# Attention and top-1 experts on one core: the common slots' rows gathered earlier and turned later

## The chip, the cores and the metric

The kernel runs on one core of a Trainium2 chip. The metric is device time in microseconds of one execution. TensorE, VectorE, ScalarE and GpSimd each work through their own list of instructions in order; SyncE and the others also issue transfers, which run on 16 DMA engines that the core's queues share.

## The reference

Attention with a memory term for 4 batches of 576 tokens and 8 heads of 64 gives x, 2304 rows of 512. Then each row goes to one of 8 experts:

```
logits = x @ w_gate;  e_idx = argmax(logits, axis=1)
for e in range(E):
    mask = e_idx == e
    h = maximum(x[mask] @ w1[e], 0)           # 512 -> 1024
    ye = h @ w2[e]                            # 1024 -> 512
    out[mask] = gate_w[mask] * eom[mask, e] * ye
```

## The kernel before

The first part (to about 226 us) computes attention and routing and writes the rows x to `xs` and their gates to `gd`, both in device memory. The second part works on **slots**: 128 rows that go to the same expert, 17 slots (`NMAIN`) in the main loop at line 1637. The change lies in that loop.

A slot `s` passes through these steps. `gather(s)` (L1365) fetches its rows from `xs` with an indirect DMA that GpSimd issues. `stage_x(s)` (L1372) turns them on TensorE (four transposes into the PSUM tile `px`, L1376), ScalarE copies them twice (`xh` rounded, `x32` as it is, L1381 and L1383), and GpSimd takes the difference `xl` (L1384). `gemm1(s)` (L1414) is the first product: 24 matmuls in four pieces `c` of six, each out of `whi*xh`, `whi*xl` and `wlo*xh` (L1405), then relu on ScalarE. `stage_h(s)` (L1421) turns the result with eight transposes (`hp`) and splits it into `hh` and `hl`, the latter again on GpSimd (L1436). `gemm2(s)` (L1439) is the second product, 24 matmuls into `py`, and an activation that weighs with the gate into `y`, one of two buffers. `scatter(s)` (L1458) writes the rows out with an indirect DMA from GpSimd. `gemm` takes a function `mid`, which it calls before the third piece, in the middle of the product (L1394): this is how transposes get into a product.

Beside the slots there are two **common slots**, numbered `kind` 0 and 1. Each holds rows of several experts: kind 0 has four groups of 32 rows, kind 1 two groups of 64, and each group is multiplied by its own expert's weights on a part of the array. `group_gather(kind)` (L1547) fetches the rows into `xc` and the gates into `gk`, two indirect DMAs of GpSimd. `group_turn(kind)` (L1554) turns the rows on TensorE (four transposes into `pc`, which takes the same PSUM buffer as `px`), and ScalarE copies them to `cx`. The work on them is cut into 24 `unit`s (L1563; the matmuls are at L1584, `ch` and `cy`), of which one follows each product from slot 2 on. Their weights come in transfers that ScalarE issues, into two buffers (`wide_load`, L1522); a unit waits for its transfer with a semaphore, and a buffer is filled again when its unit is done.

The order is written out by hand. On TensorE a pass `s` of the loop does: first product of slot `s + 1`, turn of slot `s + 2`, a unit, second product of slot `s` (with the turn `hp` of slot `s + 1` in its middle), a unit. The table `plan` (L1606) says what is put at a point `(s, half)`, after the first or the second half of pass `s`, or at `(s, "mid")`, in the middle of the first product of slot `s`. GpSimd's list follows the order in which the code calls it: at a pass's end `gather(s + 4)`, `scatter(s)`, and in passes 0 and 7 `group_gather`. The experts' weights are fetched by SyncE and split by VectorE (`load_expert`, L1335), which waits until the products of an earlier expert are done.

```
    plan[1, 1] = [lambda: group_turn(0)]
        ...
        if s + 4 < NMAIN:
            gather(s + 4, False)
        scatter(s)
        if s in (0, 7):
            group_gather(s // 7)
```

Of the kernel before, what the change touches and what calls it, by code (L numbers as in the profile page):

```python
# [10 lines left out]
F32 = mybir.dt.float32  # L11
# [9 lines left out]
P = 128  # L21
# [111 lines left out]
def attn_moe(ctx: ExitStack, tc: tile.TileContext, qk, vd, mz, mt, rz, beta, wgo, w1, w2, out):  # L133
# [236 lines left out]
    def raw_tile(name, width=F):  # L370
        tag = ("qk", "qk", "hi", "hi", "hi")[turns[0] % 5]
        turns[0] += 1
        return kq.tile([P, width], F32, name=name, tag=tag, bufs=3 if tag == "hi" else 2)
# [708 lines left out]
    for item in ORDER:  # L1082
        name, _, eng = item.partition(":")
# [168 lines left out]
    mk = fin["mk"] = ctx.enter_context(tc.tile_pool(name="mk", bufs=1, side="right"))  # L1252
# [100 lines left out]
    def gather_gate(s):  # L1353
        g = st[s]["g"] = mk.tile([P, 1], F32, name=f"g{s}", tag="g", bufs=4)
        G.indirect_dma_start(out=g, out_offset=None, in_=gd[:MID if s == "e" else NT + 1], in_offset=bass.IndirectOffsetOnAxis(ap=slot_rows(s), axis=0))
# [16 lines left out]
    def stage_x(s):  # L1372
        t = st[s]
        px = pm.tile([P, 512], F32, name=f"px{s}", tag="px")
        for c in range(4):
            T.transpose(px[:, c * P:(c + 1) * P], t["x"][:, c * P:(c + 1) * P], ident)  # L1376
        if s == 1:
            xh, xl = (mk.tile([P, DM], F32R, name=f"x{n}1", tag="y", bufs=2) for n in "hl")
        else:
            xh, xl = (mk.tile([P, DM], F32R, name=f"x{n}{s}", tag=f"x{n}") for n in "hl")  # L1380
        A.copy(xh, px)  # L1381
        x32 = mk.tile([P, DM], F32, name=f"x32_{s}", tag="x32")
        A.copy(x32, px)  # L1383
        G.tensor_tensor(xl, x32, f32(xh), op=ALU.subtract)  # L1384
        t["x1"] = xh, xl

    def regs(s):
        st[s]["need"] = T.value_load(need[0:1, s:s + 1], min_val=0, max_val=8 * E)
        st[s]["par"] = T.value_load(pari[0:1, s:s + 1], min_val=0, max_val=1)
# [24 lines left out]
    def gemm1(s, mid=None):  # L1414
        h = pa.tile([P, F], F32, name=f"h{s}", tag="h")
        gemm(s, [h[:, :512], h[:, 512:]], st[s]["x1"], 0, 2, mid)
        h32 = st[s]["h"] = bq.tile([P, F], F32, name=f"h32_{s}", tag="h32")
        A.activation(h32, h, AF.Relu)  # L1418
        done(s, sem_1)
# [38 lines left out]
    def scatter(s):  # L1458
        i = G.indirect_dma_start(out=out, out_offset=bass.IndirectOffsetOnAxis(ap=outi[:, s:s + 1] if s < NMAIN else fin["outf"][:, s - NMAIN:s - NMAIN + 1], axis=0), in_=st.pop(s)["y"], in_offset=None, bounds_check=NT - 1, oob_is_err=False)
        if s == NMAIN - 2:  # L1460
            tc.add_to_no_dep_group("rows", i.ins)


    def split(e, c, eng):
        high(e, c, eng)
        low(e, c)
        ready()
# [44 lines left out]
    cst = {}  # L1512
# [5 lines left out]
    def numbers(g0, g1):  # L1518
        for g in range(g0, g1):
            cst["e", g] = A.value_load(groupi[0:1, g:g + 1], min_val=0, max_val=E - 1)  # L1520
# [26 lines left out]
    def group_gather(kind):  # L1547
        xr = mk.tile([P, DM], F32, name=f"xc{kind}", tag="xc")
        G.indirect_dma_start(out=xr, out_offset=None, in_=xs[:NT + 1], in_offset=bass.IndirectOffsetOnAxis(ap=group_row[:, kind:kind + 1], axis=0))
        g = mk.tile([P, 1], F32, name=f"gk{kind}", tag="gk", bufs=2)  # L1550
        G.indirect_dma_start(out=g, out_offset=None, in_=gd[:NT + 1], in_offset=bass.IndirectOffsetOnAxis(ap=group_row[:, kind:kind + 1], axis=0))
        cst[kind, "x"], cst[kind, "g"] = xr, g

    def group_turn(kind):  # L1554
        px = pm.tile([P, 512], F32, name=f"pc{kind}", tag="px")
        for c in range(4):
            T.transpose(px[:, c * P:(c + 1) * P], cst[kind, "x"][:, c * P:(c + 1) * P], ident)
        if "cx" not in cst:
            cst["cx"] = raw_tile("cx")
        x = cst[kind, "cx"] = cst["cx"]  # L1560
        A.copy(x[:, :512], px)

    def unit(u):  # L1563
        kind, part, k, count = loads[u]
        b = u % 2
        T.wait_ge(sem_c[b], count)
        ng = HALVES if kind else QUARTERS
        w = P // ng
        wt = wide[b].rearrange("p (g f) -> p g f", g=ng)
        if part == 0:  # L1570
            if k == 0:
                cst[kind, "h"] = [pa.tile([P, 512], F32, name=f"ch{kind}_{n}", tag=f"c{n}") for n in range(2)]
            todo = [(cst[kind, "h"][n], k, slice(n * 512, n * 512 + 512), k == 0, k == 3) for n in range(2)] if kind else [(cst[kind, "h"][k % 2], k // 2, slice(0, 512), k < 2, k >= 6)]
            x = cst[kind, "cx"]
        else:
            if k == 0:
                cst[kind, "y"] = pa.tile([P, DM], F32, name=f"cy{kind}", tag="c0")
            o = cst[kind, "y"]
            todo = [(o, 2 * k + n, slice(n * 512, n * 512 + 512), 2 * k + n == 0, 2 * k + n == 7) for n in range(2)] if kind else [(o, k, slice(0, 512), k == 0, k == 7)]
            x = cst[kind, "cT"]  # L1580
        for o, c, z, first, last in todo:
            for g in range(ng):
                r = slice(w * g, w * g + w)
                i = apart(T.matmul(o[r], x[:, c * P + w * g:c * P + w * g + w], wt[:, g, z], start=first, stop=last, tile_position=(0, w * g)))  # L1584
        return i

    def group_relu(kind):
        x = cst[kind, "h32"] = bq.tile([P, F], F32, name=f"ch32_{kind}", tag="h32")
        for n in range(2):
            A.activation(x[:, n * 512:n * 512 + 512], cst[kind, "h"][n], AF.Relu)  # L1590

    def group_h(kind):
        hp = pa.tile([P, F], F32, name=f"chp{kind}", tag="hp")
        for f in range(8):
            T.transpose(hp[:, f * P:(f + 1) * P], cst[kind, "h32"][:, f * P:(f + 1) * P], ident)
        x = cst[kind, "cT"] = cst["cx"]
        for n in range(2):
            A.copy(x[:, n * 512:n * 512 + 512], hp[:, n * 512:n * 512 + 512])

    def group_out_rows(kind):  # L1600
        y = mk.tile([P, DM], F32, name=f"yc{kind}", tag="y", bufs=2)
        A.activation(y, cst[kind, "y"], AF.Copy, scale=cst[kind, "g"])
        G.indirect_dma_start(out=out, out_offset=bass.IndirectOffsetOnAxis(ap=group_out[:, kind:kind + 1], axis=0), in_=y, in_offset=None, bounds_check=NT - 1, oob_is_err=False)

    loads = [(0, part, k) for part in range(2) for k in range(8)] + [(1, part, k) for part in range(2) for k in range(4)]
    plan = {}  # L1606
    for i in range(24):
        s, half = divmod(i, 2)
        plan[2 + s, half] = [lambda u=i: (unit(u), None)[0]]
    plan[1, 1] = [lambda: group_turn(0)]  # L1610
    plan[5, 1].append(lambda: group_relu(0))
    plan[7, "mid"] = lambda: group_h(0)
    plan[9, 1] += [lambda: group_out_rows(0), lambda: group_turn(1)]
    plan[11, 1].append(lambda: group_relu(1))
    plan[13, "mid"] = lambda: group_h(1)
    plan[13, 1].append(lambda: group_out_rows(1))
# [2 lines left out]
    def point(s, half):  # L1619
        last = None  # L1620
        for f in plan.get((s, half), ()):
            last = f() or last
        return last

    def refill(s, half):
        if (s, half) in plan and ahead[0] < len(loads) and s >= 2:
            wide_load(ahead[0])
            ahead[0] += 1
# [8 lines left out]
    for s in range(NMAIN):  # L1637
        if 0 < s < NMAIN - 1:
            gemm1(s + 1, plan.get((s + 1, "mid")))
        if s + 2 < NMAIN:  # L1640
            stage_x(s + 2)
            regs(s + 2)
        if s == 0:
            gather_gate(0)
            wide_load(0)
        if s < NMAIN - 1:
            gather_gate(s + 1)
        if s == NMAIN - 1:
            finish(s)
            break  # L1650
        i = point(s, 0)
        refill(s, 0)
        gemm2(s, lambda: (group_rows() if s == 0 else None, stage_h(s + 1)))
        i = point(s, 1) or i
        refill(s, 1)
        if s == 13:
            tc.declare_fence(i.ins, group="wide")
        if s % 4 == 3:
            G.drain()
        if s + 4 < NMAIN:  # L1660
            gather(s + 4, False)
        scatter(s)
        if s in (0, 7):
            group_gather(s // 7)
        if s == 0:
            wide_load(1)
            for c in range(8):
                fetch(1, c)
                split(1, c, V)
        if s == 8:  # L1670
            numbers(QUARTERS, GROUPS)
        if s < NPOS - 2:
            load_expert(s + 2)
# [101 lines left out]
```

## Time and profile before

| | |
|---|---|
| median of 3 runs | 484.91 us (484.63 to 485.42) |
| profiled execution | 484.58 us |
| its span | 482.9 us |
| mean granted clock of TensorE | 0.989 |
| busy share: TensorE, VectorE, ScalarE, GpSimd | 96%, 58%, 54%, 55% |

The span runs from the first to the last instruction; all times within it count from its start. The profiled execution is one of its own, beside the three runs, and 1.68 us of its time lie outside the span. An engine is busy while it executes; waits for a semaphore are idle time, and the view of waits puts each down to what ended it. The chain is followed back from the last instruction. "Issue" is idle time that ended without a visible wait. The DMA engines' share can read a little over 1.

### The profile page before, as it was taken

The numbers are of one execution on the slowest core, as the hardware profiler recorded it, in microseconds if no ns is written. First come the engines' busy times: TensorE is split into PE (matmuls) and PEld (weight loads), VectorE is DVE, ScalarE is ACT, GpSimd is POOL, SyncE is SP. The second block draws the span as 40 slices with busy tenths as digits, with TensorE's granted clock in tenths as the row PEclk, the third lists the DMA queues.
The fourth block names the chain that finished last, engine by engine and source line by source line (L and its number), as shares of the span: only waits on it lengthen the run. The fifth ranks groups of instructions, "written<-read, shape, count | busy, mean of one in ns | idle before, by whom it ended". The sixth has DMA issues, their size and how long they took to land.

```text
span 482.9 us, 10479 instructions
## 1 busy us (share of the span) xinstructions
PE 465.7 (96%) x3315; PEld 348.3 (72%) x3315; DVE 282.1 (58%) x847; ACT 262.6 (54%) x621; POOL 266.2 (55%) x264
## 2 busy tenths in 40 slices
PE   7999999999999999989996999999999999999994
PEld 4777877877877877646885677676676767676884
DVE  4978998989789978888995707007079700000000
ACT  5989898888878766345342423344233332523341
POOL 8846585544745742634587445454478653452452
PEclk9999999999999999999997999999999999999998
DMA  7544256243221271151598686858779745341001
GB/s 252 178 137 138 74 183 198 80 133 142 87 90 35 92 224 48 55 197 48 179 367 294 202 286 209 317 168 266 263 247 369 278 142 209 132 159 59 36 22 40
DMA packets 34215, 80.09 MB, mean 166 GB/s; under 512 B 4820, under 2 KB 5352, under 8 KB 34154
## 3 DMA queue, kind: packets, MB, share of 16 engines
q1 hardware_dynamic: 17610, 44.05, 27.3%
q10 hardware_dynamic: 12688, 25.30, 15.3%
q0 software_dynamic: 3856, 9.98, 6.0%
q8 instruction: 32, 0.52, 0.5%
q14 instruction: 29, 0.24, 0.1%
HBM read 69.86 MB, written 9.97 MB: 165 GB/s over the span
## 4 chain that ended last, share of the span: by engine, by line
PE 88%; DVE 3%; DMA 2%; issue 2%; ACT 1%; POOL 1%; POOLq 0%; SPq 0%; DVEq 0%; ACTq 0%
PE h L1405 20%; PE py L1405 17%; PE po L675 9%; PE pt L640 8%; PE s L565 7%; PE me L731 4%; PE cy L1584 3%; PE ch L1584 3%; PE hp L1431 3%; PE sd L552 3%; PE pt L609 2%; DMA xc<-xs,group_row 1%; PE px L1376 1%; PE pv L794 1%; PE pl L899 1%
## 5 line engine op out<-in xcount | busy, mean ns | idle before, releaser
L1436 POOL TENSOR_TENSOR hl<-hT,hh 128x512 fp32r<-128x512 f32 x32 | 45.8, 1454 | 52.1 <-ACT hh L1435 52.1
L628 ACT ACTIVATE st<-st,nm 128x128 f32<-128x128 f32 (+3 forms) x128 | 71.5, 562 | 3.5 <-DVE nm L623 3.2
L1098 DVE CAST whi<-kept 128x1024 fp32r<-128x1024 f32 x32 | 32.7, 1022 | 67.4 <-ACTq L1412 59.8
L623 DVE CUSTOM_DVE_ANT_0 st<-s,mask 128x128 f32<-128x128 f32 (+3 forms) x128 | 58.3, 483 | 9.4 <-PE s L565 5.4
L1405 PE MATMUL h<-whi,xh 128*128 (+1 forms) x136 | 56.7, 417 | 0.0
L460 POOL TENSOR_TENSOR lo<-qk,hi 128x1216 fp32r<-128x1216 f32 x15 | 42.2, 2811 | 23.2 <-ACT hi L456 17.7
L1405 PE MATMUL h<-whi,xl 128*128 (+1 forms) x136 | 54.0, 397 | 0.0
L487 ACT COPY PT<-pt 128x512 f32<-128x512 f32 (+2 forms) x89 | 45.3, 523 | 15.9 <-PE pt L640 13.8
L1405 PE MATMUL h<-wlo,xh 128*128 (+1 forms) x136 | 53.9, 396 | 0.0
L1405 PE MATMUL py<-whi,hh 128*128 (+1 forms) x128 | 53.0, 414 | 0.0
L1418 ACT ACTIVATE h<-h 128x1024 f32<-128x1024 f32 x17 | 17.4, 1026 | 63.5 <-PE h L1405 63.5
L1405 PE MATMUL py<-wlo,hh 128*128 (+1 forms) x128 | 50.2, 392 | 0.0
L1405 PE MATMUL py<-whi,hl 128*128 (+1 forms) x128 | 50.0, 391 | 0.0
L675 PE MATMUL po<-PT,v 128*64 128x320 f32 (+4 forms) x480 | 49.1, 349 | 0.8 <-ACT oT_hT L487 0.4
L640 PE MATMUL pt<-ident,st 128*128 128x128 f32 x320 | 47.7, 280 | 0.1
L1434 ACT COPY hT<-hp 128x512 f32<-128x512 f32 x34 | 20.1, 590 | 49.6 <-PE hp L1431 49.6
L1384 POOL TENSOR_TENSOR xl<-x,xh 128x512 fp32r<-128x512 f32 x17 | 23.5, 1383 | 41.6 <-ACT x L1383 40.6
L1101 DVE TENSOR_TENSOR wlo<-kept,whi 128x1024 fp32r<-128x1024 f32 x32 | 45.1, 1411 | 1.1
L675 PEld LDWEIGHTS po<-PT,v 128*64 128x64 f32 x480 | 29.6, 137 | 17.7 <-issue 2.8
L640 PEld LDWEIGHTS pt<-ident,st 128*128 128x128 f32 x320 | 35.2, 141 | 7.1 <-issue 1.9
L1435 ACT CAST hh<-hp 128x512 fp32r<-128x512 f32 x32 | 19.1, 596 | 32.3 <-PE py L1405 32.3
L1405 PEld LDWEIGHTS h<-whi,xh 128*128 128x128 f32 x136 | 26.1, 192 | 14.6 <-ACT hh L1435 9.1
(337 smaller groups left out, 1025.3 us busy)
## 6 DMA issues: line engine op xcount, KB each, us to landing
kept<-in_w SPq DMA_DIRECT2D x32, 512.0 KB
wide<-in_w ACTq DMA_DIRECT2D x64, 256.0 KB
qk<-in_qk SPq DMA_DIRECT2D x15, 640.0 KB
wide<-in_w ACTq DMA_DIRECT2D x16, 512.0 KB
v<-in_vd SPq DMA_DIRECT2D x16, 320.0 KB
xs<-xd SPq DMA_DIRECT2D x12, 256.0 KB
star<-in_w SPq DMA_DIRECT2D x6, 512.0 KB
mz<-in_mz SPq DMA_DIRECT2D x4, 324.0 KB
```

The lines of the kernel that those rows point to most:

```text
L460: G.tensor_tensor(c["lo"][:, TQ:], c["raw"][:, TQ:], f32(c["hi"])[:, TQ:], op=ALU.subtract)
L487: (A.copy if e == "ACT" else V.tensor_copy)(dst(), src())
L565: T.matmul(c()["ss", q][j], l[r, lc], m[r, KC:KC + w], start=(a == 0), stop=(a == 2))
L623: V.tensor_tensor_reduce(st[:, :w], c()["ss", qt][j], mask[:, 512 - w:512], -SCALE, 3.0e38, ALU.add, ALU.min, negm()[:, i:i + 1])
L628: A.activation(st, st, AF.Exp, bias=c()["negm"][:, i:i + 1], scale=-1.0, accum_out=sums()[:, qt, 2 * p + j:2 * p + j + 1])
L640: T.transpose(pt[:, (m * k1 + i) * P:(m * k1 + i + 1) * P], st[:, i * P:(i + 1) * P], ident)
L675: T.matmul(po[64 * j:64 * j + 64, qs - q0:q1 - q0], vt[:, k, 64 * j:64 * j + 64], PT[:, j, k, qs:q1], start=(k == 0), stop=(k == kn - 1))
L1098: join((A.copy if eng is A else eng.tensor_copy)(whi[:, e % 2, c, :], raws[e, c]))
L1101: join(eng.tensor_tensor(wlo[:, e % 2, c, :], raws.pop((e, c)), f32(whi[:, e % 2, c, :]), op=ALU.subtract))
L1405: i = T.matmul(o[n % nh], l[:, z], m[:, n * 512 + part.start:n * 512 + part.stop], start=(c == 0 and k == 0 and n < nh), stop=(c == 3 and ...
L1436: G.tensor_tensor(hl[:, z], hT[:, z], f32(hh)[:, z], op=ALU.subtract)
L1584: i = apart(T.matmul(o[r], x[:, c * P + w * g:c * P + w * g + w], wt[:, g, z], start=first, stop=last, tile_position=(0, w * g)))
```

## The change

In passes 0 and 8 (before: 0 and 7) the rows of a common slot are gathered first in the pass's list of GpSimd, ahead of `gather(s + 4)`. Their gates are gathered by a function of their own, two passes later, in passes 2 and 10. Slot 0's scatter moves from the end of pass 0 into pass 1, behind `stage_x(3)`. The turns move from the end of passes 1 and 9 into the middle of the first products of slots 3 and 11, which passes 2 and 10 begin with. No instruction is added or removed.

```diff
--- before.py
+++ after.py
@@ -1547,9 +1547,11 @@
     def group_gather(kind):
         xr = mk.tile([P, DM], F32, name=f"xc{kind}", tag="xc")
         G.indirect_dma_start(out=xr, out_offset=None, in_=xs[:NT + 1], in_offset=bass.IndirectOffsetOnAxis(ap=group_row[:, kind:kind + 1], axis=0))
-        g = mk.tile([P, 1], F32, name=f"gk{kind}", tag="gk", bufs=2)
+        cst[kind, "x"] = xr
+
+    def group_gate(kind):
+        g = cst[kind, "g"] = mk.tile([P, 1], F32, name=f"gk{kind}", tag="gk", bufs=2)
         G.indirect_dma_start(out=g, out_offset=None, in_=gd[:NT + 1], in_offset=bass.IndirectOffsetOnAxis(ap=group_row[:, kind:kind + 1], axis=0))
-        cst[kind, "x"], cst[kind, "g"] = xr, g
 
     def group_turn(kind):
         px = pm.tile([P, 512], F32, name=f"pc{kind}", tag="px")
@@ -1607,10 +1609,11 @@
     for i in range(24):
         s, half = divmod(i, 2)
         plan[2 + s, half] = [lambda u=i: (unit(u), None)[0]]
-    plan[1, 1] = [lambda: group_turn(0)]
+    plan[3, "mid"] = lambda: group_turn(0)
     plan[5, 1].append(lambda: group_relu(0))
     plan[7, "mid"] = lambda: group_h(0)
-    plan[9, 1] += [lambda: group_out_rows(0), lambda: group_turn(1)]
+    plan[9, 1].append(lambda: group_out_rows(0))
+    plan[11, "mid"] = lambda: group_turn(1)
     plan[11, 1].append(lambda: group_relu(1))
     plan[13, "mid"] = lambda: group_h(1)
     plan[13, 1].append(lambda: group_out_rows(1))
@@ -1640,6 +1643,8 @@
         if s + 2 < NMAIN:
             stage_x(s + 2)
             regs(s + 2)
+        if s == 1:
+            scatter(0)
         if s == 0:
             gather_gate(0)
             wide_load(0)
@@ -1657,11 +1662,14 @@
             tc.declare_fence(i.ins, group="wide")
         if s % 4 == 3:
             G.drain()
+        if s in (0, 8):
+            group_gather(s // 8)
         if s + 4 < NMAIN:
             gather(s + 4, False)
-        scatter(s)
-        if s in (0, 7):
-            group_gather(s // 7)
+        if s:
+            scatter(s)
+        if s in (2, 10):
+            group_gate(s // 8)
         if s == 0:
             wide_load(1)
             for c in range(8):
```

GpSimd's list at the end of pass 0, before. `xr` are a slot's gathered rows (slot 4 here), `out<-y` is a scatter, `xc` and `gk` are the common slot's rows and gates, `g` a slot's gate, `xl` and `hl` the differences.

```order
L1436 TENSOR_TENSOR hl_4000<-hT_3998,hh_3999 128x512 x2
L1367 DMA xr_4032<-xs,rowi_3514 128x512
L1459 DMA out<-y_4029,outi 2304x512
L1549 DMA xc_4037<-xs,group_row 128x512
L1551 DMA gk_4039<-gd,group_row 128x1
L1384 TENSOR_TENSOR xl_4180<-x_3_4182,xh_4179 128x512
L1355 DMA g_4203<-gd,rowi_3513 128x1
L1436 TENSOR_TENSOR hl_4224<-hT_4222,hh_4223 128x512 x2
```

The same place after the change:

```order
L1436 TENSOR_TENSOR hl_4000<-hT_3998,hh_3999 128x512 x2
L1549 DMA xc_4032<-xs,group_row 128x512
L1367 DMA xr_4034<-xs,rowi_3514 128x512
L1384 TENSOR_TENSOR xl_4175<-x_3_4177,xh_4174 128x512
L1459 DMA out<-y_4029,outi 2304x512
L1355 DMA g_4201<-gd,rowi_3513 128x1
L1436 TENSOR_TENSOR hl_4222<-hT_4220,hh_4221 128x512 x2
L1367 DMA xr_4252<-xs,rowi_3514 128x512
L1459 DMA out<-y_4249,outi 2304x512
```

The gather into `xc` goes from fourth to second row and `xl` from sixth to fourth; the scatter is now behind `xl`, and `gk` is out of this stretch.

TensorE's list where slot 1's second product (`py`) ends and slot 3's first (`h`) begins, before; `pc` are the transposes of the common slot's rows. "ISA" and "REGISTER_ALU" rows set registers.

```order
L1405 MATMUL py_4205<-wlo,hh_3999 128x512
L1557 MATMUL pc_4254<-ident,xc_4037 128x128 x4
L1400 REGISTER_ALU
L1405 ISA
L1405 MATMUL h_4318<-whi,xh_4179 128x512
L1405 ISA
L1405 MATMUL h_4318<-whi,xl_4180 128x512
```

After the change, in the middle of slot 3's first product, behind its twelfth matmul:

```order
L1405 MATMUL h_4309<-whi,xl_4175 128x512
L1405 ISA
L1405 MATMUL h_4309<-wlo,xh_4174 128x512
L1559 MATMUL pc_4325<-ident,xc_4032 128x128 x4
L1405 ISA
L1405 MATMUL h_4309<-whi,xh_4174 128x512
```

The product now begins right behind `py`, and `pc` stands between its halves.

## Rows read from the trace of the kernel before

**Rows 1.** The page: the span, busy time, and the granted clock in 40 slices.

```profile
span 482.9 us, 10479 instructions
...
PE 465.7 (96%) x3315; PEld 348.3 (72%) x3315; DVE 282.1 (58%) x847; ACT 262.6 (54%) x621; POOL 266.2 (55%) x264
...
PEclk9999999999999999999997999999999999999998
```

**Rows 2.** Waits of TensorE, 226 us to the end: us in total, times, longest.

```profile
PE pc L1557 <- DMA xc<-xs,group_row: 3.9, 1, 3.9
```

**Rows 3.** Timeline of TensorE: start, us, what, idle time before it.

```profile
253.59 0.39 PE L1405 MATMUL py<-whi,hl 128*128 x1
253.81 0.39 PE L1405 MATMUL py<-wlo,hh 128*128 x1
258.15 1.08 PE L1557 MATMUL pc<-ident,xc 128*128 128x128 f32 x4 [3.94 <-DMA xc<-xs,group_row]
```

**Rows 4.** Timeline of GpSimd around the first gather, and one gather later.

```profile
242.75 3.62 POOL L1436 TENSOR_TENSOR hl<-hT,hh 128x512 fp32r<-128x512 f32 x2 [1.83 <-ACT hh L1435]
246.52 1.88 POOL L1367 DMA_INDIRECT xr<-xs,rowi  x1 [0.15 <-issue]
248.71 1.79 POOL L1459 DMA_INDIRECT out<-y,outi  x1 [0.30 <-ACT h L1418]
250.80 1.78 POOL L1549 DMA_INDIRECT xc<-xs,group_row  x1 [0.30 <-issue]
252.89 1.65 POOL L1551 DMA_INDIRECT gk<-gd,group_row  x1 [0.30 <-issue]
254.56 1.29 POOL L1384 TENSOR_TENSOR xl<-x,xh 128x512 fp32r<-128x512 f32 x1
...
307.69 0.96 POOL L1367 DMA_INDIRECT xr<-xs,rowi  x1
```

**Rows 5.** The chain that ended last, around the wait: start, us, what.

```profile
250.80 7.21 DMA xc<-xs,group_row
...
259.23 7.56 PE h L1405 x24
266.79 0.44 PE px L1376 x4
...
275.79 5.67 PE h L1405 x24
```

**Rows 6.** Windows: us; busy PE, PEld, DVE, ACT, POOL; granted clock, DMA share, GB/s.

```profile
255.00:256.00 1.00, 0.00 (x0) 0.00 (x0) 0.79 (x1) 1.00 (x3) 0.84 (x1) 1.00 1.05 420
257.00:258.00 1.00, 0.00 (x0) 0.00 (x0) 0.86 (x2) 0.00 (x0) 0.98 (x2) 0.50 1.04 410
261.00:262.00 1.00, 1.00 (x3) 0.73 (x3) 0.59 (x1) 0.00 (x0) 1.00 (x1) 0.50 0.02 8
264.00:265.00 1.00, 1.00 (x6) 0.82 (x5) 0.00 (x0) 0.00 (x0) 0.00 (x0) 1.00 0.97 393
```

**Rows 7.** The chain at slot 7's first product and at the second turn.

```profile
319.85 2.96 PE h L1405 x12
322.81 0.87 PE chp L1595 x8
323.68 2.75 PE h L1405 x12
...
379.49 0.59 PE pc L1557 x4
380.08 5.47 PE h L1405 x24
```

**Rows 8.** Timeline of ScalarE: slot 3's rows copied for `xl`.

```profile
249.14 0.59 ACT L1383 COPY x<-px 128x512 f32<-128x512 f32 x1
```

**Rows 9.** Timeline of VectorE: the first cast for the third expert.

```profile
268.05 0.69 DVE L1098 CAST whi<-kept 128x1024 fp32r<-128x1024 f32 x1 [6.46 <-ACTq L1412]
```

**Rows 10.** Windows, same columns: the fullest 14 us of the DMA engines.

```profile
366.00:380.00 14.00, 14.00 (x77) 10.02 (x76) 11.60 (x11) 4.16 (x8) 8.51 (x6) 1.00 0.99 360
```

## The prediction

> **What bounds the kernel now.** I read the page first, then the waits of TensorE, then the order of time on TensorE and GpSimd around the one wait that is left, then the chain. The page says that TensorE is busy for 96% of a 482.9 us span, and one digit of its clock row, the 22nd of 40 slices, is a 7 among nines (the 8 at the row's end is the end of the work) [rows 1]. The waits of TensorE after 226 us have one line: its matmuls stood still once, for 3.9 us, at the transposes `pc`, for the transfer into `xc` [rows 2]. So from 226 us on a change is worth what it does to TensorE's own line of work, and nothing on another engine costs anything until TensorE waits for it.
>
> The timeline shows the place [rows 3]: the last matmul of slot 1's second product starts at 253.81; with the 0.22 us from one start to the next, the next could have started at about 254.04; `pc` starts at 258.15. GpSimd's list shows why [rows 4]: after the `hl` of slot 1, which ends at 246.37, it issues the gather of slot 4 (246.52), slot 0's scatter (248.71) and only then the gather into `xc` (250.80). The chain carries that gather as 7.21 us, to 258.01 [rows 5]. The wait has a second price. The granted clock is 1.00 at 255 to 256 us, 0.50 (1.2 instead of 2.4 GHz) at 257 to 258 and at 261 to 262, and 1.00 again at 264 to 265 [rows 6]: TensorE stood idle before it fell and had worked for some 5 us when it was back. The 24 matmuls of slot 3's first product take 7.56 us in the chain under it, and 5.67 for slot 4 at full clock [rows 5].
>
> **The change part by part.**
> *The first turn moves into the product.* Before, from 254.04 to the transposes `px` of slot 4 (266.79 [rows 5]) TensorE spends 12.75 us: 4.11 idle, 1.08 for `pc`, 7.56 for the product. After, with xc there in time, it spends 5.67 for the product and the price of four transposes inside one. For that there is a row: the first product of slot 7 has eight transposes in its middle and takes 2.96 + 0.87 + 2.75 = 6.58 [rows 7], 0.91 more than 5.67, so four cost about 0.45. 12.75 - 6.12 = 6.63 us saved: 4.11 of idle time, 0.63 on `pc`, and 1.89 on the product.
> *The second turn* stands between products today, without a wait: 0.59 + 5.47 = 6.06 [rows 7]. Inside the product the same work is 6.12: 0.06 lost.
> *The gather goes ahead.* It takes the place of slot 4's gather in GpSimd's list, 250.80 - 246.52 = 4.28 us earlier. Its latency isn't known for the new place. Bounds: it can't be under its 1.78 us on GpSimd [rows 4]; at the old one it was 7.21, with two other gathers or scatters just ahead of it and the DMA engines at a share of 1.05 [rows 6]. I take 7.21, which is of the same queue, 4 us on, under the same load: it lands at 253.73. The turn needs it at 254.04 + 2.96 = 257.00. Margin 3.3 us. If that cover were gone, TensorE would wait again, inside the product.
> *What is late next: `xl` of slot 3.* The second matmul of that product reads it. Today it waits behind four DMA issues on GpSimd and ends at 254.56 + 1.29 = 255.85 [rows 4], hidden by the longer wait for xc. Had the turn alone been moved, the product would have stood until then, for about 1.6 us (255.85 - 254.27). After, two issues are ahead of it: xc (246.52, 1.78, and 0.30 to the next), slot 4's gather (248.60, 1.88, and 0.15), so xl starts at 250.63, when its input from ScalarE is there (249.14 + 0.59 [rows 8]), and ends at 251.92, 2.3 us before it is read. That is why slot 0's scatter had to go behind it.
> *Slot 0's scatter* is issued about 3.5 us later (251.92 + 0.30 against 248.71). Behind it stand the gate of slot 2 and the `hl` of slot 2; they have two issues fewer ahead of them than today, and so come sooner. The y buffer that the scatter reads is one of two, and its next writer is the activation of slot 2, which comes after slot 3's first and slot 2's second product, over 12 us on: free. The cost if this cover were gone is ScalarE's wait, which TensorE would feel one slot later.
> *Slot 4's gather* goes 2.1 us later and is read at `px` of slot 4, at 260.2: 11 us. Free. *The two gates* each put one issue of about 1.65 us [rows 4] ahead of an `xl` in slots 2 and 10. TensorE waits for no xl anywhere today [rows 2], so I cost them at nothing; if one were uncovered it would cost its 1.65 + 0.30. SP's queue and ScalarE's transfers of weights keep their order.
> *Everything behind comes earlier by the same time*, since TensorE runs back to back from there to its last product, and the weights' transfers are released by it. VectorE's casts of the next expert show this: the one at 268.05 waited 6.46 us for a product's end [rows 9].
>
> Sum: -6.63 + 0.06 = -6.57. Against the profiled execution (484.58 us, of which 482.9 is the span) that is 478.0, with a span of 476.3; against the median of the runs, which is 0.33 above the profiled one, 478.3. I predict **478.2**.
>
> **The rivals.**
> *The wait moves into the product.* If xc is still out at 257.00, TensorE stops there. What speaks for it: GpSimd's issues take 1.78 to 1.88 here, beside VectorE's casts of weights, and 0.96 in a quiet stretch [rows 4], and the DMA engines are full. Against: the 7.21 was measured under the same. The Trainium skill, "SBUF — State Buffer", section "A bandwidth-pool intuition that's wrong (but worth ruling out)", says that a GpSimd-issued DMA beside a VectorE copy waits for the shared port, 3.1 us where it takes 0.62 alone. The trace agrees in kind and shows less than a factor of 2; by the page's factor of 5 the estimate for the issue is 4.8, xc lands at 256.75, and the sum stays, with hardly a margin. From rows alone: a landing at 257 + w costs w, and once w is near the 3.9 us after which the clock is seen to fall, the 1.89 too. It decides against the change from w = 4.7 on (4.7 + 1.9 = 6.6), a latency of 15 us, twice the measured one. With a latency of 10.5 to 15 us the time is between 478.2 and 484.8; with 17 us, w = 6.5, it is 478.2 + 6.5 + 1.9 = 486.6, **slower**. Chance 0.04 for a part of the gain, 0.02 for slower.
> *The time is given back later.* TensorE comes 6.6 us earlier to weights, and the engines are full at times (share 0.99 over 366 to 380 [rows 10]). If a transfer there were already just in time, the whole gain would return as a wait: 484.9, no change. Against: no other wait of TensorE exists after 226 us, two units' weights were asked for long before they are read (at 261 to 262 the DMA engines are nearly empty, 0.02 [rows 6], so both have landed), and later ones are asked for when TensorE frees the buffer, so the distance stays. Chance 0.04.
> *The clock doesn't come back with the wait.* If the fall at 256 us has another cause than the idle time, the 1.89 stays and the time is 480.1. For it: nothing but that it happened once here. Against: it is 1.00 before and after, in products of the same kind. The Trainium skill, "TensorE: Matmul & The Clock Gate", section "What's actually happening", says that the half rate is the state without recent work and that work releases it; by it the clock stays up, and the trace agrees. Chance 0.05.
> *The change doesn't do what it says*: no sign; the lists of the changed kernel show the gather at the head of its slot's list and the turn in the middle of a product. Chance under 0.01.
>
> **How the numbers follow.** The forecast has 0.85. Its own spread is the three runs' (-0.3, +0.5) and about 0.4 on the four transposes and the clock: 477.3 to 479.2. To hold 8 in 10 it would do alone; I take in the third rival's 480.1, and end at 480.3. A measurement of this kernel can tell about 0.2% (1 us) from no change. Faster by more than that: forecast, partial wait and clock, 0.85 + 0.04 + 0.05 = 0.94, less 0.01 for the unforeseen: 0.93. Within it: 0.04. Slower: 0.02 and 0.01 for the unforeseen.
>
> **What would show it.** Right: TensorE's list of waits after 226 us has no line for `pc`; the gather into xc starts near 246.5; slot 3's first product starts near 254.0 and is in two halves of under 3 us around four transposes; the clock row has no 7 there; `px` of slot 4 is at 260.2, and the span is 476.3. Wrong: a wait for xc or xl inside that product, a granted clock under 1.00 in it, or a new wait of the units (`ch`, `cy`) for their weights between 260 and 450 us.

## The result, and the profile after

The changed kernel takes 478.81 us (median of 4 runs, 478.11 to 479.62); the kernel before, on the same occasions, 485.17 (484.63 to 486.58). The ratio is 0.9869, with a 95% interval of 0.9843 to 0.9894: 6.4 us faster. The prediction was 478.2, range 477.3 to 480.3. The profiled execution took 479.24 us, with a span of 477.4. Among the executions of the later occasions two stand far outside, 787.86 us of the kernel with the gather put late and 909.96 us of the kernel before; the ratios and intervals leave them out and are not simply quotients of the medians.

The page answers to [rows 1]:

```profile
span 477.4 us, 10482 instructions
...
PE 465.1 (97%) x3315; PEld 347.9 (73%) x3315; DVE 283.8 (59%) x847; ACT 262.6 (55%) x621; POOL 266.0 (56%) x264
...
PEclk8999999999999999999999999999999999999998
```

TensorE's share is a point higher in a shorter span. The page counts three instructions more than before (10482 against 10479); the engines' counts of busy ones are the same. The 7 in the clock row is gone; the granted clock of a microsecond in the middle of slot 3's product (columns as in [rows 6]) is 1.00:

```profile
257.00:258.00 1.00, 1.00 (x8) 0.83 (x7) 1.00 (x1) 0.33 (x1) 1.00 (x1) 1.00 1.00 399
```

The first digit of the row is now an 8, which it was not before; that is a matter of the first 12 us, where nothing was changed (last section).

The waits of TensorE from 226 us on, to compare with [rows 2], are an empty list, of which only the head is there:

```profile
engine line waited for: us in total, times, longest us
```

GpSimd's timeline, to compare with [rows 4] (start, us, what, idle time before it):

```profile
247.56 1.88 POOL L1549 DMA_INDIRECT xc<-xs,group_row  x1
249.75 1.78 POOL L1367 DMA_INDIRECT xr<-xs,rowi  x1 [0.30 <-ACT h L1418]
251.56 1.28 POOL L1384 TENSOR_TENSOR xl<-x,xh 128x512 fp32r<-128x512 f32 x1
253.01 1.87 POOL L1459 DMA_INDIRECT out<-y,outi  x1 [0.17 <-issue]
```

The gather into `xc` is the first of the issues, at 247.56, and no longer the third. `xl` of slot 3 ends at 251.56 + 1.28 = 252.84, behind two issues. TensorE's timeline of the same place, for [rows 3]:

```profile
254.93 0.39 PE L1405 MATMUL h<-whi,xh 128*128 x1
255.15 0.39 PE L1405 MATMUL h<-whi,xl 128*128 x1
...
257.42 0.39 PE L1405 MATMUL h<-wlo,xh 128*128 x1
257.65 0.60 PE L1559 MATMUL pc<-ident,xc 128*128 128x128 f32 x4
...
260.84 0.60 PE L1376 MATMUL px<-ident,xr 128*128 128x128 f32 x4
```

Slot 3's first product starts at 254.93. Its second matmul, which reads `xl`, comes at 255.15, 2.3 us after xl's end. The four transposes start 0.23 us after the twelfth matmul, so xc was there in time. How early it landed is shown by the view of the DMA issues from 247 to 249 us, whose last column is the time from issue to landing:

```profile
xc<-xs,group_row POOLq DMA_INDIRECT x1, 7.9
```

It landed at 247.56 + 7.9 = 255.5, which is 2.2 us before the transposes and 0.5 us after the start of the product. The chain has the same stretch and the second turn, for [rows 5, 7]:

```profile
255.09 2.72 PE h L1405 x12
257.81 0.44 PE pc L1559 x4
258.25 2.76 PE h L1405 x12
261.01 0.44 PE px L1376 x4
...
373.70 2.96 PE h L1405 x12
376.66 0.44 PE pc L1559 x4
377.10 2.75 PE h L1405 x12
```

The product's halves take 2.72 and 2.76 us around 0.44 for the transposes.

**A measure that the rest of the run doesn't touch.** The spans of single executions differ by more than the experiments below were to tell apart. So I use, beside the times, the stretch from the start of slot 3's transposes `px` to the start of slot 4's, from the timeline of TensorE: it holds slot 1's second product, slot 3's first one, the first turn, and every wait in question. Its two ends before the change, and its first end after it:

```profile
247.20 0.60 PE L1376 MATMUL px<-ident,xr 128*128 128x128 f32 x4
266.63 0.60 PE L1376 MATMUL px<-ident,xr 128*128 128x128 f32 x4
```

```profile
248.09 0.60 PE L1376 MATMUL px<-ident,xr 128*128 128x128 f32 x4
```

The stretch of a kernel is read from its one profiled execution; times and ratios are from all runs, each ratio against the runs of the kernel before on the same occasion.

| kernel | px of slot 3, us | px of slot 4, us | stretch, us | median time, us | ratio to before beside it (95%) |
|---|---|---|---|---|---|
| before | 247.20 | 266.63 | 19.43 | 485.17 | |
| changed | 248.09 | 260.84 | 12.75 | 478.81 | 0.9869 (0.9843 to 0.9894) |
| changed, again | 248.43 | 261.18 | 12.75 | 478.89 | 0.9875 (0.9837 to 0.9913) |
| turns alone | 248.45 | 262.11 | 13.66 | 480.60 | 0.9923 (0.9893 to 0.9954) |
| GpSimd's list alone | 251.12 | 263.88 | 12.76 | 479.48 | 0.9878 (0.9844 to 0.9912) |
| scatter left in pass 0 | 247.02 | 259.77 | 12.75 | 479.61 | 0.9899 (0.9860 to 0.9937) |
| first common slot alone | 247.40 | 260.15 | 12.75 | 478.37 | 0.9873 (0.9821 to 0.9925) |
| gather put late | 247.81 | 267.96 | 20.15 | 485.64 | 1.0017 (0.9987 to 1.0047) |
| before, with work in the wait | 247.51 | 264.99 | 17.48 | 482.94 | 0.9966 (0.9936 to 0.9995) |

With it the span of the changed kernel is accounted for: 6.68 shorter in the stretch; 0.89 later at its start (248.09 against 247.20); 0.09 longer at the second turn (2.96 + 0.44 + 2.75 = 6.15 against 6.06 [rows 7]); and 0.18 longer from the last instruction of the chain to the end of the span. -6.68 + 0.89 + 0.09 + 0.18 = -5.52, and the spans differ by 482.9 - 477.4 = 5.5.

### The profile page after: what moved, and what is told of

Same layout as the page of the kernel before. It is cut to its first block, busy times and chain, and to the rows that moved or that the text cites. A ratio compares the mean times of both kernels' runs of the same rounds, so it can differ in the third digit from the quotient of the medians.

```text
span 477.4 us, 10482 instructions
## 1 busy us (share of the span) xinstructions
PE 465.1 (97%) x3315; PEld 347.9 (73%) x3315; DVE 283.8 (59%) x847; ACT 262.6 (55%) x621; POOL 266.0 (56%) x264
## 4 chain that ended last, share of the span: by engine, by line
PE 91%; DVE 3%; POOL 2%; issue 2%; POOLq 0%; ACT 0%; DVEq 0%; ACTq 0%
PE h L1405 20%; PE py L1405 18%; PE po L675 10%; PE pt L640 8%; PE s L565 7%; PE me L731 4%; PE cy L1586 3%; PE ch L1586 3%; PE hp L1431 3%; PE sd L552 3%; PE pt L609 2%; PE px L1376 2%; PE pv L794 1%; PE pl L899 1%; PE pye L1130 1%
## 5 line engine op out<-in xcount | busy, mean ns | idle before, releaser
L1098 DVE CAST whi<-kept 128x1024 fp32r<-128x1024 f32 x32 | 30.0, 938 | 59.4 <-ACTq L1412 50.8
L1101 DVE TENSOR_TENSOR wlo<-kept,whi 128x1024 fp32r<-128x1024 f32 x32 | 49.2, 1537 | 1.1
```

What stands on the lines that cost most here:

```text
L1098: join((A.copy if eng is A else eng.tensor_copy)(whi[:, e % 2, c, :], raws[e, c]))
L1101: join(eng.tensor_tensor(wlo[:, e % 2, c, :], raws.pop((e, c)), f32(whi[:, e % 2, c, :]), op=ALU.subtract))
```

## The experiments

Theory: TensorE's own line is all that counts here; the gain is the idle time, what the clock lost behind it, and nothing else; it needs xc by the turn and xl by the product's second matmul. Rivals: one half of the change alone brings it; or the wait goes into the product; or the clock fell for another reason.

**The turns alone.** GpSimd's list is that of the kernel before:

```diff
-    plan[1, 1] = [lambda: group_turn(0)]
+    plan[3, "mid"] = lambda: group_turn(0)
...
-    plan[9, 1] += [lambda: group_out_rows(0), lambda: group_turn(1)]
+    plan[9, 1].append(lambda: group_out_rows(0))
+    plan[11, "mid"] = lambda: group_turn(1)
```

> Only the two turns move into the products; GpSimd's list is that of the kernel before. Theory (TensorE's line from 254 us on is all that counts, and the product needs xl by its second matmul and xc by its middle): xl of slot 3 still ends behind four issues, at about 255.9, the product stands 1.6 us at its second matmul, its middle comes at 258.6, just after xc (258.0), and the clock stays at 1.00: 485.2 - 6.4 + 1.6 = 480.4 us. Rival A (the turn alone does it): no wait, 478.8. Rival B (the wait for xc moves into the product): a wait at the transposes of over 1 us, 481.5 or more.

It took 480.60 us (8 runs). GpSimd's timeline, then TensorE's, in this kernel:

```profile
247.99 1.24 POOL L1367 DMA_INDIRECT xr<-xs,rowi  x1
249.54 1.07 POOL L1459 DMA_INDIRECT out<-y,outi  x1 [0.31 <-issue]
250.92 1.78 POOL L1549 DMA_INDIRECT xc<-xs,group_row  x1 [0.30 <-issue]
253.01 1.79 POOL L1551 DMA_INDIRECT gk<-gd,group_row  x1 [0.30 <-issue]
254.82 1.29 POOL L1384 TENSOR_TENSOR xl<-x,xh 128x512 fp32r<-128x512 f32 x1
```

```profile
255.29 0.39 PE L1405 MATMUL h<-whi,xh 128*128 x1
256.16 0.50 PE L1405 MATMUL h<-whi,xl 128*128 x1 [0.49 <-POOL xl L1384]
...
258.88 0.63 PE L1557 MATMUL pc<-ident,xc 128*128 128x128 f32 x4
```

The wait is where the theory puts it, at the second matmul, for `xl`, and the list has none for xc. But it is 0.49 us long, not 1.6: the first two issues took 1.24 and 1.07 us here, against 1.88 and 1.79 in [rows 4], and the product came 1.2 us later in the span, while xl ended at about the same time (254.82 + 1.29 = 256.11 against 255.85). In the stretch the kernel loses 0.91 against the changed one. So in this profile the turn alone brings 5.77 of 6.68 us (19.43 - 13.66), and rivals A and B both fall, A by little. That the median comes to the 480.4 expected is in part luck: the wait is a third of the one in the sum, 0.91 us in the stretch is less than the 1.7 us between 480.60 and the 478.89 of the changed kernel beside it, and the two intervals overlap.

**GpSimd's list alone.** The changed kernel with the two turns back between the products:

```diff
-    plan[3, "mid"] = lambda: group_turn(0)
+    plan[1, 1] = [lambda: group_turn(0)]
...
-    plan[9, 1].append(lambda: group_out_rows(0))
-    plan[11, "mid"] = lambda: group_turn(1)
+    plan[9, 1] += [lambda: group_out_rows(0), lambda: group_turn(1)]
```

> Only GpSimd's list changes; both turns stay between the products. Theory: xc lands 7.2 us after its issue, at the time at which the transposes come (254.8 against 254.9 in the trace of the changed kernel), so TensorE waits for under 0.5 us or not at all and the clock stays up: 478.8, within 0.5. Rival (the turn had to move too, because the gather is slower when it is issued earlier): a wait of over 1 us at the transposes, 479.8 or more.

It took 479.48 us. The gather's row on GpSimd, and TensorE's timeline (the row at 257.73 is the second product's last matmul):

```profile
249.85 1.88 POOL L1549 DMA_INDIRECT xc<-xs,group_row  x1 [0.15 <-issue]
```

```profile
257.73 0.39 PE L1405 MATMUL py<-wlo,hh 128*128 x1
257.96 0.60 PE L1559 MATMUL pc<-ident,xc 128*128 128x128 f32 x4
```

The transposes follow the matmul ahead of them by 0.23 us, as in a row without a wait: xc landed in under 257.96 - 249.85 = 8.11 us. The stretch is 12.76, so in this profile the new order of GpSimd's list does by itself what the whole change does; the rival falls. Which of the list's three moves does it (the gather, the scatter or the gates) this run doesn't separate. And its margin is thin. Here the transposes come 8.11 us after the issue; in the changed kernel they would come, at the start of the product, 254.93 - 247.56 = 7.37 us after it, and xc took 7.9. In the three other profiles that show a landing at this place (the changed kernel's third measurement, the first common slot alone, the work at the start) it took 8.2, 8.2 and 8.5, and the product started 8.12, 7.73 and 8.12 us after the issue. So without the move of the turn an estimate from these four rows is a wait of 0.1 to 0.5 us, too little for the medians to tell (479.48 against 478.89). The span of this profile is longer for what lies ahead of the stretch, which starts at 251.12: the granted clock is 0.50 at 218 to 220 us, behind 1.48 us of idle time, and TensorE waits 0.62 us for an `hl` at 238.83.

**The scatter left where it was.** The changed kernel with slot 0's scatter at the end of pass 0:

```diff
-        if s == 1:
-            scatter(0)
...
-        if s:
-            scatter(s)
+        scatter(s)
```

> The changed kernel with slot 0's scatter left in pass 0, between slot 4's gather and xl of slot 3. The prediction said that it had to go. By the trace of the changed kernel xl then ends at 253.0 + 1.87 + 0.15 + 1.28 - 0.9 (one row earlier), about 255.2, and is read at 255.15. Theory: a wait of 0 to 0.3 us on TensorE, 478.8 to 479.1. Rival (the scatter's place carries part of the gain): a wait of over 0.8 us at the second matmul, 479.6 or more.

It took 479.61 us, with a stretch of 12.75. GpSimd's scatter and xl, then the second matmul of TensorE's product:

```profile
250.26 1.79 POOL L1459 DMA_INDIRECT out<-y,outi  x1 [0.30 <-issue]
252.08 1.30 POOL L1384 TENSOR_TENSOR xl<-x,xh 128x512 fp32r<-128x512 f32 x1
```

```profile
254.08 0.39 PE L1405 MATMUL h<-whi,xl 128*128 x1
```

xl ends at 253.38 and is read at 254.08. The cover is 0.7 us, thinner than the 2.3 of the changed kernel, but TensorE doesn't wait. In this profile the theory holds, and the prediction's sentence that the scatter had to move does not; by the issue times of the changed kernel (1.87 + 0.30 more ahead of xl) 0.14 us of cover would be left. The median lies at the rival's 479.6 and not in the theory's 478.8 to 479.1. But the six runs go from 477.98, the profiled one, to 482.35, and their interval holds the changed kernel's ratio. So the times decide nothing here, and the trace, which shows no wait, is that of one execution.

**The changed kernel again, on the chip of the three above.**

> The changed kernel itself, on the chip of the three others, as their measure: 6.4 us under the kernel before, no wait of TensorE after 226 us. Rival (its gain was partly the chance of the first runs, whose spans differ by 1.4 us): under 5.5 us.

478.89 us against 484.93, 6.0 less, and the same stretch of 12.75: the gain isn't a chance of the first runs.

**The first common slot alone.** The second one's gathers and its turn stay in their old places:

```diff
-    plan[9, 1].append(lambda: group_out_rows(0))
-    plan[11, "mid"] = lambda: group_turn(1)
+    plan[9, 1] += [lambda: group_out_rows(0), lambda: group_turn(1)]
...
-        if s in (0, 8):
-            group_gather(s // 8)
+        if s == 0:
+            group_gather(0)
...
-        if s in (2, 10):
-            group_gate(s // 8)
+        if s == 7:
+            group_gather(1)
+        if s in (2, 7):
+            group_gate(s // 7)
```

> The change for the first common slot alone; the second one's gathers and turn stay where the kernel before has them. Theory (the second had no wait to lose, and four transposes cost about 0.1 more inside a product): 478.8 - 0.1 = 478.7, and no wait of TensorE after 226 us. Rival (the second part of the change carries something, or costs something): 0.5 us or more to either side, with a wait near 380 us.

478.37 us, stretch 12.75, no wait of TensorE after 226 us. The chain at the second turn:

```profile
373.01 0.59 PE pc L1559 x4
373.60 5.47 PE h L1405 x24
```

That is 6.06 us, as before the change [rows 7], and 0.09 less than in the changed kernel: in these profiles the second part of the change costs a tenth of a microsecond and brings nothing. In the medians that cannot be seen.

**The gather put late.** To make the rival happen, the first gather goes behind slot 0's scatter and slot 2's gate:

```diff
+        if s == 1:
+            group_gather(0)
...
-        if s in (0, 8):
-            group_gather(s // 8)
+        if s == 8:
+            group_gather(1)
```

> The changed kernel with the first gather put late: behind slot 0's scatter and slot 2's gate in GpSimd's list, so that it is issued near 256.3 instead of 247.2 us. It makes the rival of the prediction happen (xc still out in the middle of the product). Theory: the latency is again about 7.2, xc lands near 263.5, TensorE stops for about 5.5 us behind the twelfth matmul, the granted clock falls and the rest runs slowly for another 1.9: 478.8 + 7.4 = 486.2 us, no better than the kernel before. Rival A (the clock stays, since the product has just run): 484.3. Rival B (a latency of 3 to 4 us, since fewer transfers are out then): a wait of 2 us, 480.8.

It took 485.64 us. TensorE's timeline (the twelfth matmul and the transposes), the chain, and three windows of the clock (columns as in [rows 6]):

```profile
257.13 0.39 PE L1405 MATMUL h<-wlo,xh 128*128 x1
262.85 1.08 PE L1559 MATMUL pc<-ident,xc 128*128 128x128 f32 x4 [5.32 <-DMA xc<-xs,group_row]
```

```profile
256.61 6.10 DMA xc<-xs,group_row
...
263.93 4.19 PE h L1405 x12
```

```profile
259.00:260.00 1.00, 0.00 (x0) 0.00 (x0) 1.00 (x1) 0.00 (x0) 1.00 (x2) 1.00 1.02 287
261.00:262.00 1.00, 0.00 (x0) 0.00 (x0) 0.99 (x1) 0.00 (x0) 0.94 (x1) 0.50 0.78 315
267.00:268.00 1.00, 1.00 (x6) 0.75 (x5) 0.00 (x0) 0.00 (x0) 0.00 (x0) 1.00 0.00 0
```

The gather lands 6.10 us after its issue. TensorE stands still for 5.3 us in the middle of the product, the granted clock falls to 0.50, and the second half takes 4.19 us where it takes 2.76 in the changed kernel. The stretch is 7.40 us longer than the changed kernel's and 0.72 longer than the one before; the ratio, 1.0017 (0.9987 to 1.0047), is no change. Rival A (the clock stays) and rival B (a short latency) fall.

**Work in the wait.** The kernel before, with 16 matmuls on constants ahead of the first turn's transposes; they write the buffer that the transposes then overwrite:

```diff
         px = pm.tile([P, 512], F32, name=f"pc{kind}", tag="px")
+        for _ in range(0 if kind else 16):
+            T.matmul(px.rearrange("p (a c) -> p a c", c=P), ones, ones.unsqueeze(1).to_broadcast([P, 4, P]), start=True, stop=True)
```

> The kernel before, with 16 matmuls of 512 columns on constants into the buffer of the first turn, just ahead of its transposes: about 3.7 us of work in the 4.1 us of idle time, the gather and the turn where they were. It computes the same. Theory (the clock fell because TensorE was idle): the wait for xc at the transposes shrinks to under 0.6 us, the granted clock stays at 1.00, pc takes 0.6 and slot 3's first product 5.7 us: 485.2 - 1.9 - 0.5 = 482.8. Rival (the fall has another cause): the clock falls at 256 us as before and the time stays at 485.2.

482.94 us, against 485.73 beside it. TensorE's timeline, the chain, and the clock:

```profile
254.35 3.63 PE L1557 MATMUL pc<-ones 128*128 128x512 bf16 x16
259.01 0.66 PE L1559 MATMUL pc<-ident,xc 128*128 128x128 f32 x4 [1.04 <-DMA xc<-xs,group_row]
```

```profile
251.17 7.80 DMA xc<-xs,group_row
...
259.67 5.48 PE h L1405 x24
```

```profile
258.00:259.00 1.00, 0.00 (x0) 0.00 (x0) 0.86 (x2) 0.00 (x0) 1.00 (x1) 1.00 0.70 247
260.00:261.00 1.00, 1.00 (x6) 0.82 (x5) 1.00 (x1) 0.29 (x1) 0.86 (x1) 1.00 0.81 328
```

xc lands no sooner (7.80 us after its issue), but the clock stays at 1.00, the transposes take 0.66 instead of 1.08 and the product 5.48 instead of 7.56. So it was the idle time that had lowered the clock, and work without any use holds it up. The runs beside the profile go the same way: 8 of 10 have a mean clock of 0.994 or more, against 6 of the 18 of the kernel before. The stretch is 1.95 us shorter than before, where 2.4 were expected: xc came 7.80 us after its issue and not 7.21, which left a wait of 1.04. The medians differ by 2.8, and the interval of the ratio leaves room for 0.2 to 3.1. The Trainium skill, "TensorE: Matmul & The Clock Gate", section "What's actually happening", says that work releases the half rate; this run agrees, at a clock of 1.00.

**Work in the wait at the start.** The spans of one kernel differ by up to 3.5 us from run to run (476.3 to 479.8 for the changed kernel again), and the mean clocks with them (0.999 to 0.990). I tried the same means on the first idle stretch of TensorE, in the kernel with the first common slot alone:

```diff
-... M0_1_0 SS0_3 SS0_2 ...
+... M0_1_0 fill1 fill2 fill3 fill4 SS0_3 SS0_2 ...
```

> The change for the first common slot alone, and 12 matmuls of 256 columns on constants behind the first scores, where TensorE stands idle from 6.8 to 8.3 us: about 1.3 us of work beside the computation. It asks what the rest of the spread between runs is. Theory (the same kernel's spans of 476.3 to 479.8 differ by whether the granted clock falls near 9 us, behind that idle time): it stays at 1.00 there, the mean clock is 0.996 or more in nearly all runs, and the median is 477.5 to 478.3, about 1 us under the changed kernel beside it. Rival (the spread has another cause): the same mean clocks, 0.990 to 0.999, and the same median.

> The changed kernel once more, as the measure for the start fill on the same chip: 478.8, with mean clocks of 0.990 to 0.999 and the spans falling as the clock rises.

Medians of 478.43 and 478.58 us, ratios 0.9852 (0.9829 to 0.9876) and 0.9854 (0.9831 to 0.9877). The mean clocks were 0.996 to 0.999 with the work and 0.997 to 0.999 without: by these clocks the fall at the start came in no run of either, and the stretch is 12.75 in both profiles. So the run doesn't tell whether the work would have prevented it. It is no worse, and no version here beats the changed kernel by what a measurement shows.

## Why the prediction was right

- *The first turn, 6.63.* Measured in the stretch: 6.68. Two errors of the sum cancel, which is luck. Its 12.75 runs from a start of the timeline to a start of the chain; from start to start in the timeline it is 266.63 - 254.04 = 12.59, since the idle time is the 3.94 of the wait and not 4.11. Its 6.12 took 5.67 for the product at full clock; measured are 5.48 for the two halves and 260.84 - 254.93 = 5.91 for the whole. So the terms are 3.94 of idle time, 1.08 - 0.44 = 0.64 on the transposes, as forecast, and 7.56 - 5.48 = 2.08 for the clock, where 1.89 was forecast. The kernel with work in the wait shows the clock's part by itself: 2.08 on the product and 0.42 on the transposes, with the gather and the turn where they were.
- *The second turn, 0.06 lost.* Measured: 0.09.
- *xc in time for the middle of the product, by 3.3 us.* It was in time, by 2.2 us: the latency was 7.9 us at the new place, and 8.2 to 8.5 in the three other profiles that show it. Those that were waited for, of gathers issued at 250.80, 251.17 and 256.61, are 7.21, 7.80 and 6.10. So the old one was too short for the new place by 0.7 to 1.3 us, and the cover hid it.
- *xl next, 2.3 us before it is read.* Measured: 2.3. That the turn alone would leave a wait of 1.6 was too much: the wait is there, with 0.49 us. The step took GpSimd's issues at the 1.8 to 1.9 us of [rows 4]; two of them took 1.1 to 1.2 in that run, although VectorE was at work through nearly all of both.
- *"That is why slot 0's scatter had to go behind it."* This step failed, as far as one profile shows. With the scatter in its old place xl still ends 0.7 us before it is read. With three issues ahead of it instead of four, xl is already in time, if barely by the issue times of the changed kernel; the prediction had worked out two and four, and not three.
- *The halves of the change.* The prediction added both up into one margin (4.28 us earlier, 2.96 later) against a wait of 4.11 and didn't ask whether one would do. Either nearly would: in their profiles GpSimd's list alone gives all of the gain and the turns alone 5.77 of 6.68 us. The two are not terms of a sum but two ways to the same end; what the turn adds to the list is cover, worth 0.1 to 0.5 us by the landings.
- *The rival in the product.* Its price was w + 1.9, against the change from w = 4.7 on. With the gather put late w was 5.3 and the loss 7.4 in the stretch, 0.72 more than the gain. The price comes out near, 7.2, by terms that offset each other: the clock cost 4.19 - 2.76 = 1.43 on the half product that was left, and 1.08 - 0.44 = 0.64 on the transposes, which the price had left out. One w doesn't test the point; it agrees with it. The clock was at 0.50 before the wait was over, here and in [rows 6], so the prediction's "3.9 us after which" it falls is the length of a wait and no bound. The Trainium skill, "SBUF — State Buffer", section "A bandwidth-pool intuition that's wrong (but worth ruling out)", gave an estimate of 4.8 us for the issue beside VectorE's casts; the trace of the changed kernel has 1.88 for it, under twice the 0.96 of a quiet stretch [rows 4]. That the trace agrees in kind holds as a range: of GpSimd's indirect DMAs from 230 us on in the kernel before, the 31 issued while VectorE stood still held GpSimd for 0.96 to 1.03 us, and the 19 issued while it was busy for over 80% of their time for 0.98 to 1.88.
- *Given back later; the clock from another cause.* Neither: the list of waits is empty, and work in the wait held the clock.
- *The span, 476.3.* It was 477.4, with 0.89 of the difference already there when the stretch begins. Without that part the forecast for the span is met within 0.2 us.

## What to carry to other kernels

Where a stage waits for a transfer, first look at what stands ahead of its issue in the queue: here two issues cost TensorE 6.7 us, and reordering the queue alone got nearly all of it back. When an edit makes something both earlier and needed later, test each half by itself, and read from the landing how much cover each leaves: a part without a wait to cover can be given up again (here the whole second part), while one that leaves a few tenths of cover (the scatter in its old place) is better kept. And price an idle stretch of TensorE with the slow work behind it, 2 to 2.5 us in this case beside 4 us of idle time.

## What the runs showed of the hardware that I had not expected

The fall of the granted clock behind an idle stretch isn't the same in every execution. Two profiles of the changed kernel, TensorE's first long scores and a window of 1 us behind them (columns as in [rows 6]), the first with a fall, the second, of the third measurement, without:

```profile
8.33 0.50 PE L565 MATMUL s<-lo,hi 64*128 64x512 f32 x2 [1.49 <-POOL lo L472]
```

```profile
10.00:11.00 1.00, 1.00 (x7) 0.57 (x4) 0.88 (x4) 0.97 (x3) 0.83 (x2) 0.50 1.04 406
```

```profile
8.62 0.50 PE L565 MATMUL s<-lo,hi 64*128 64x512 f32 x2 [2.22 <-POOL lo L472]
```

```profile
10.00:11.00 1.00, 1.00 (x10) 0.96 (x9) 1.00 (x5) 0.76 (x3) 1.00 (x2) 1.00 1.13 411
```

The idle time was 1.49 us in the one and 2.22 in the other, and it is the shorter one behind which the clock is 0.50. Two more profiles with a fall there have 1.60 us (the changed kernel again, GpSimd's list alone), and two without have 2.45 and 2.50 (the kernel before, the gather put late). In the kernel with GpSimd's list alone the clock also fell behind 1.48 us of idle time at 217 us, where the changed kernel kept it behind 1.38. So the length of the idle time alone doesn't decide; what does, no run here shows. By the mean clocks it moves whole runs: of 13 runs of the kernel before that stood beside the first four experiments, two have spans of 480.5 and 480.6 us with a mean clock of 0.998, and the slowest 485.6 with 0.988. The former are 4.1 to 4.2 us over the shortest span of the changed kernel (476.4 in its first runs, at 0.996), which is the idle time without the clock's part. That reading rests on spans and mean clocks alone; there is no trace of such a run.
